# Hourglass attention and a gated feed-forward on one core: batch 0's attention given a fourth PSUM tile, and four smaller edits

## The chip, the cores and the metric

One of the eight cores of a Trainium2 chip runs the whole program. The time is the device's own, in microseconds, from start to end of one execution. The engines are PE (matrix multiply, with its weight loads PEld), ScalarE (ACT), VectorE (DVE), GpSimd (POOL) and SyncE (SP, here only a queue that issues DMAs). Matmul results go to PSUM, 8 banks of 128 partitions x 512 fp32, and are taken from there by ScalarE or VectorE.

## What is computed

q, k and v have 8 batches, 8 heads, 576 tokens and 64 dimensions. Each head gets two attentions, a "down" one over tokens averaged by four (144 x 144) and a local one with a band mask, and their sum goes through a feed-forward of 512 to 2048 to 512 on 4608 tokens:

```python
q_d = q.reshape(B, H, Sd, factor, D).mean(axis=3)
k_d = k.reshape(B, H, Sd, factor, D).mean(axis=3)
v_d = v.reshape(B, H, Sd, factor, D).mean(axis=3)
out_d = sm_attn(q_d, k_d, v_d)
out_up = np.repeat(out_d, factor, axis=2)
...
mask = np.abs(pos[:, None] - pos[None, :]) < factor
scores = scale * np.matmul(q, k.transpose(0, 1, 3, 2))
scores = np.where(mask, scores, -1000000000.0)
...
out_local = np.matmul(attn, v)
return (out_up + out_local).astype(np.float32)
...
h = x @ w_in
g = h * (1.0 / (1.0 + np.exp(-1.702 * h)))
return (g @ w_out).astype(np.float32)
```

Here `sm_attn` is scaled softmax attention, `attn` the softmax of the masked scores, and x the attention's result with the heads side by side.

## The kernel before

The program is written in the order in which each engine is to run it; nothing is reordered. Waits between engines are derived from the tiles that the instructions read and write.

**Batch 0 first (lines 922 to 1018).** No feed-forward work exists yet, so batch 0's attention stands alone. POOL loads q, k and five chunks of v (`load_vb0`, one DMA each, casting to bf16), then, behind a one-element copy `gate` that waits for chunk 1, the weights w_in. PE runs warming matmuls on zeros (`warm`), writes the mask as additive bars (`bars0`), adds scores (`scores0`, heads in quads `qd` 0 and 1), and ScalarE takes the exp (`exp0`). `scores_d` makes the down scores and `exp_down` their exp. `prep_vd_pe` sums v by four with matmuls into PM[0] and PM[1], and VectorE casts the result. Per pair of heads `hp`, `av_local0` and `av_down0` multiply with v into `o[hp]`, `normalise0` divides on VectorE, `transp_sum` turns y with matmuls and sums both attentions, and `copy_x` takes x to SBUF on ScalarE.

**PSUM.** Three tiles PA of two banks each (called PB in another order) and two tiles PM of one bank. Before, `o` uses PB[0], PB[1], PB[2] and again PB[0]; x of pair 0 is turned into the two PM tiles, of pairs 1, 2, 3 into PB[1], PB[2], PB[0]. The first feed-forward matmuls (`part`, `acc`, `late`) then take banks as they come free.

**Groups 0 to 7 (`mm1`, `mm2`).** Each group is 512 tokens. `mm1` makes 16 blocks `ffc` of 128 hidden columns, four matmuls of 128x512 each, into a list of banks, and `silu` (L817) takes each block out on ScalarE. From group 2 on the banks run PM[0], PA, PM[1], PA, PA, and again so, and the last six blocks alternate between PM[0] and PM[1]. Group 1 begins with both halves of two PA tiles. `mm2` sums 16 matmuls per block `t` of 128 tokens into alternating PM tiles (L884), and `store` copies each block out on ScalarE (L869) and sends it from SP's queue. In group 0 blocks 0 and 1 run abreast in the two PM tiles, and 2 and 3 in PB[0].

**Attention of batch g+1** runs inside group g as steps at set places of these loops (`POS`, and `POS_0` for group 0; place n below 16 is before block n of mm1, from 16 on before matmul n-16 of mm2). Step 0 makes scores of quad 0 (`s_pe`), step 1 their exp and mask (`s_act`), step 2 both for quad 1, steps 3 and 4 `avx` for heads (0,1) and (2,3): matmuls into the PA tiles, then Ln and exp on ScalarE (L739 to L745), copies and products on VectorE. Group 0 has four steps `avx1` in place of two.

```python
PA = [psum.tile([128, 2, 512], FP32, name=f"pa{i}") for i in range(3)]
PM = [psum.tile([128, 512], FP32, name=f"pm{i}") for i in range(2)]
two = [PA[i][:, u, :] for i in range(3) for u in range(2)]
bank, abreast = [PM[0], two[0], PM[1], two[2], two[4]], 4
bank = bank + bank + PM + PM + PM
```

Of the kernel before, what the change touches and what calls it, by code (L numbers as in the profile page):

```python
# [8 lines left out]
FP32 = mybir.dt.float32  # L9
# [10 lines left out]
def kernel(  # L20
# [9 lines left out]
    nc = tc.nc  # L30
    B, H, S, D = q.shape
# [22 lines left out]
    psum = ctx.enter_context(  # L54
        tc.tile_pool(name="psum", bufs=1, space=bass.MemoryType.PSUM)
    )
# [6 lines left out]
    vbs = [persist.tile([128, 5, H, 65], BF16, name=f"vb{i}") for i in range(2)]  # L63
# [4 lines left out]
    for _ in range(2):  # L68
        t = work.tile([128, 2 * (S + SD)], FP32, name="l", tag="l", bufs=2).bitcast(BF16)
# [2 lines left out]
    kdT = [persist.tile([128, 160, 2], BF16, name=f"kdT{i}") for i in range(NQ)]  # L72

    PA = [psum.tile([128, 2, 512], FP32, name=f"pa{i}") for i in range(3)]
    PM = [psum.tile([128, 512], FP32, name=f"pm{i}") for i in range(2)]
    PB = [PA[2], PA[0], PA[1]]
    turn = {"a": 2, "m": 0}

    def pm_tile():
        turn["m"] += 1  # L80
        return PM[turn["m"] % 2]

# [93 lines left out]
    def make_up():  # L176
        nc.scalar.copy(out=up, in_=id128[:, :, None].to_broadcast([128, 128, 4]))
# [78 lines left out]
            )  # L256

    def load_vb0(i):
        n = min(128, S - 114 * i)
        nc.gpsimd.dma_start(  # L260
            out=vbs[0][0:n, i, :, 0:D],
            in_=bass.AP(
                tensor=v.tensor, offset=v[0, 0].offset + 114 * i * D,
                ap=[[D, n], [S * D, H], [1, D]],
            ),
        )

    def load_v4(b):
        for kc in range(3):
# [20 lines left out]
    def load_w_out(c):  # L290
        nc.gpsimd.dma_start(
            out=w_out_bf[:, 4 * c : 4 * c + 4, :],
            in_=bass.AP(
                tensor=moe_w_out.tensor, offset=moe_w_out.offset + c * 512 * d_model,
                ap=[[d_model, 128], [128 * d_model, 4], [1, d_model]],
            ),
        )
# [74 lines left out]
    def prep_vd_pe(b, pv, kcs=range(3), eng=None, between=None):  # L372
        vb, vd = vbs[b], vds[b]

        def heads(x, j):
            if b == 0:
                return x.rearrange("p (hp j) d -> p hp j d", j=2)[:, :, j]
            return x.rearrange("p (m u j) d -> p m u j d", m=2, u=2)[:, :, j]

        for kc, iis in ((0, (0, 1)), (1, (1, 2, 3)), (2, (3, 4))):  # L380
            if kc not in kcs:
                continue
            c0 = 256 * (kc - kcs[0])
            for i in iis:
                if between:
                    between(kc, i)
                for j in range(2):
                    nc.tensor.matmul(
                        pv[64 * j : 64 * j + 64, c0 : c0 + D * HP],
                        lhsT=psel[b][i // 4][:, PSEL_AT[i, kc] : PSEL_AT[i, kc] + 64],  # L390
                        rhs=heads(vb[:, i, :, 0:D], j),
                        start=(i == iis[0]), stop=(i == iis[-1]),
                        tile_position=(0, 64 * j),
                    )
        cp = eng.tensor_copy if eng else nc.scalar.copy
        cp(
            out=vd[:, kcs[0] : kcs[-1] + 1, :, 0:D],
            in_=pv[:, 0 : 256 * len(kcs)].rearrange(
                "p (k h d) -> p k h d", k=len(kcs), h=HP
            ),  # L400
        )


    def bank0(r, i):
        if i < 4:
            return PB[r // 2][:, r % 2, Q0 * i : Q0 * i + Q0]
        return (PB[2][:, r, 0:Q0] if r < 2 else PM[r - 2][:, 0:Q0])

# [50 lines left out]
    def scores_d(b, qd, sd=None, rounds=range(6)):  # L459
        bank = [sd[:, u, :] for u in range(2)]  # L460
        for n in rounds:
            kc, a = n // 2, n % 2
            for r in range(4):
                rows = slice(32 * r, 32 * r + 32)
                u, j = (r // 2, r % 2) if b < 1 else (r % 2, r // 2)
                nc.tensor.matmul(  # L466
                    bank[u][64 * j : 64 * j + 64, SD * kc : SD * kc + SD],
                    lhsT=kdT[qd][rows, 48 * kc : 48 * kc + 64, a],
                    rhs=qdT[b, qd][rows, :, a],
                    start=(a == 0), stop=(a == 1),  # L470
                    tile_position=(32 * r, 64 * j),
                )
        return sd
# [8 lines left out]
    def exp0(qd):  # L482
        def part(u, j, i, x):
            out = ez[qd][:, u, :, i, 0:Q0] if j is None else ez[qd][:, u, j, i, 0:Q0]
            nc.scalar.activation(out=out, in_=x, func=AF.Exp, scale=inv_sqrt_d)

        def most(u):
            part(u, None, slice(0, 4), PB[u][:, :, 0 : 4 * Q0].rearrange(
                "p j (i c) -> p j i c", c=Q0))

        part(1, 0, 4, PM[0][:, 0:Q0])
        if qd:
            part(1, 1, 4, PM[1][:, 0:Q0])
            most(0)
# [4 lines left out]
        if not qd:  # L499
            part(1, 1, 4, PM[1][:, 0:Q0])  # L500

    def exp_down(qd, sd):
        nc.scalar.activation(  # L503
            out=eds[qd][:, :, 0:432], in_=sd[:, :, 0:432],
            func=AF.Exp, scale=inv_sqrt_d / 16.0,
        )
# [6 lines left out]
    def av_local0(hp, o, chunks):  # L513
        for i in chunks:
            for j in range(2):
                nc.tensor.matmul(
                    o[:, j, 65 * i : 65 * i + 65],
                    lhsT=ez[hp // 2][:, hp % 2, j, i, :],
                    rhs=vbs[0][:, i, 2 * hp + j, :],
                    start=True, stop=True,  # L520
                )

    def av_down0(hp, o):
        Ed, vd, u = eds[hp // 2], vds[0], hp % 2
        for c in range(2):
            for kc in range(3):
                q0 = SD * kc + 16 * c
                for j in range(2):
                    nc.tensor.matmul(
                        o[:, j, 65 * (5 + c) : 65 * (6 + c)],  # L530
                        lhsT=Ed[64 * j : 64 * j + 48, u, q0 : q0 + 128],
                        rhs=vd[64 * j : 64 * j + 48, kc, hp, :],
                        start=(kc == 0), stop=(kc == 2),
                        tile_position=(64 * j, 0),
                    )

    def y_tiles0():
        return (
            work.tile([128, 7, 2, D], BF16, name="y", tag="y", bufs=4),
            work.tile([128, 2, 7, 1], FP32, name="rc0", tag="rc0", bufs=4),  # L540
        )
# [228 lines left out]
    def warm(n, cols=512, t=None):  # L770
        t = pm_tile() if t is None else t
        for _ in range(n):
            nc.tensor.matmul(
                t[:, 0:cols], lhsT=wz[:, 0:128], rhs=wz[:, 0:cols], start=True, stop=True
            )
# [37 lines left out]
    def new_gT():  # L813
        return moe_sb.tile([128, n_ffc, TG], BF16, name="gT", tag="gT")
# [6 lines left out]
    def mm1(g, gT, steps):  # L821
        two = [PA[i][:, u, :] for i in range(3) for u in range(2)]
        bank, abreast = [PM[0], two[0], PM[1], two[2], two[4]], 4
        if g == 0:
# [85 lines left out]
        for f in steps.get(n, ()):  # L910
            f()

    POS = [12, 16, 35, 43, 54]
    POS_0 = [16, 18, 28, 40, 49, 58, 67]
    VDP_0 = 36

    o, y, x = {}, {}, {}
# [13 lines left out]
    for i in range(5):  # L931
        load_vb0(i)
# [6 lines left out]
        load_qk(1, qd)  # L939
    load_w_out(0)  # L940
    load_w_out(1)
    warm(11)
    make_up()
    make_psel0()
    prep_1("k", 0, 0)
# [25 lines left out]
    scores0(1, 4, (0, 1))  # L971
    exp0(1)
    for hp in range(4):
        o[hp] = PB[hp % 3]
        y[hp] = y_tiles0()
    prep_vd_pe(0, PM[0], (0, 1), eng=nc.vector)
    av_local0(0, o[0], range(3))
    prep_vd_pe(0, PM[1], (2,), eng=nc.vector)
    av_local0(0, o[0], range(3, 5))
    av_local0(1, o[1], range(5))  # L980
    for hp in range(4):
        if hp == 2:
            exp_down(1, scores_d(0, 1, PB[2]))
        if hp > 1:
            av_local0(hp, o[hp], range(5))
        av_down0(hp, o[hp])
        normalise0(o[hp], y[hp])
    make_dm()
    make_mask()
    gT0 = new_gT()  # L990
    acc = PM + [PB[n][:, u, :] for n in (1, 2, 0) for u in range(2)]
    late = [acc[n] for n in (0, 1, 6, 2, 4, 0, 1, 0, 1, 0)]

    def part(ffcs, *dmcs):
        for dmc in dmcs:
            for ffc in ffcs:
                hps_mm(0, ffc, dmc, acc[ffc])

    def turned(hp, n):
        x = PM if n is None else [PB[n][:, u, :] for u in range(2)]  # L1000
        transp_sum(y[hp], x)
        copy_x(0, hp, x)

    turned(0, None)
    turned(1, 1)
    part((0, 1), 0)
    turned(2, 2)
    part((0, 1), 1)
    part((2, 3), 0)
    turned(3, 0)  # L1010
    nc.scalar.preload_act_table_set("silu_and_others")
    part((2, 3), 1)
    part((0, 1, 2, 3), 2)
# [5 lines left out]
    for g in range(n_groups):  # L1019
# [32 lines left out]
        if b < B:  # L1052
            for n, f in zip(POS if g else POS_0, attention(b)):
                steps.setdefault(n, []).append(f)
# [35 lines left out]
```

## Time and profile before

| what | value |
|---|---|
| three runs | 313.64, 313.80, 314.07 us (median 313.80) |
| profiled execution, its own time | 313.58 us |
| its span, first to last instruction | 311.8 us |
| granted PE clock, mean | 1.000 |
| PE matmul 128x512 in L884, mean | 379 ns, one every 216 ns |
| SiLU from PM (L817), mean | 604 ns |
| output copy (L869), mean with its smaller forms | 582 ns |
| first 24.2 us: PE busy | 19.6 us |
| 24.2 to 281.0 us: PE busy | all but 0.07 us |

In the page and the timeline a row gives the start, the length, the engine, the line, what is written and read, how many instructions are merged, and in brackets the engine's idle time before it and what ended that. Matmuls overlap in PE's pipeline: one lasts 379 ns, but the next starts 216 ns after it.

### The profile page before, as it was taken

What the parts mean: (1) busy time and instruction counts of PE and PEld (TensorE: products, weight loads), DVE (VectorE), ACT (ScalarE), POOL (GpSimd) and SP (SyncE); (2) the same over time, 40 slices, a digit from 0 to 9 for tenths busy, and PEclk for the clock granted to TensorE, in tenths of its full rate; (3) what the DMA queues carried; (4) which work ended last, traced back from release to release, by engine and by line L of the source; (5) the groups of instructions that cost most, each with busy time, mean ns of one, the idle gap of its engine ahead of it and who ended that gap; (6) DMA issues with size and microseconds to landing.
All of it is one profiled execution on the core that took longest, in us unless ns stands there. A gap on an engine that the chain in (4) does not pass through costs nothing.

```text
span 311.8 us, 9642 instructions
## 1 busy us (share of the span) xinstructions
PE 303.6 (97%) x4182; PEld 156.6 (50%) x4182; DVE 149.7 (48%) x304; ACT 203.3 (65%) x327; POOL 148.7 (48%) x169
## 2 busy tenths in 40 slices
PE   8789999999999999999999999999999999999995
PEld 3464554674644555455545554555455544444444
DVE  5984937761495059605980389028912770000000
ACT  4737766787767777667866895589558857316611
POOL 8552294295238943795359733983397210000000
PEclk9999999999999999999999999999999999999999
DMA  6999999899537941696159715991430110010011
GB/s 108 135 208 210 182 117 211 218 237 227 139 108 181 201 126 68 177 214 155 46 176 197 191 39 159 189 204 63 133 92 33 39 69 0 34 67 36 0 67 67
DMA packets 64042, 39.93 MB, mean 128 GB/s; under 512 B 44544, under 2 KB 54912, under 8 KB 64000
## 3 DMA queue, kind: packets, MB, share of 16 engines
q0 software_dynamic: 18784, 14.94, 34.2%
q1 hardware_dynamic: 45072, 24.32, 27.8%
q8 instruction: 32, 0.52, 0.7%
q10 hardware_dynamic: 144, 0.07, 0.1%
q14 instruction: 10, 0.08, 0.1%
HBM read 44.81 MB, written 9.44 MB: 174 GB/s over the span
## 4 chain that ended last, share of the span: by engine, by line
PE 92%; DMA 3%; POOL 2%; issue 1%; DVE 1%; ACT 1%; POOLq 0%; DVEq 0%; ACTq 0%
PE pm L884 37%; PE pm L806 25%; PE pa L806 16%; PE pa L439 3%; DMA vb<-in_v_dram 3%; PE pa L884 2%; PE pa L696 2%; PE pa L674 2%; PE pa L466 2%; PE pm L899 1%; POOL vb L260 1%; DVE y L547 1%; PE pa L609 1%; PE pa L567 0%; PE pa L597 0%
## 5 line engine op out<-in xcount | busy, mean ns | idle before, releaser
L884 PE MATMUL pm<-w_out_bf,gT 128*128 128x512 bf16 x528 | 119.4, 379 | 0.0
L806 PEld LDWEIGHTS <-w_in_bf 128*128 128x128 bf16 x612 | 59.2, 98 | 63.1 <-issue 0.3
L806 PE MATMUL pm<-xT,w_in_bf 128*128 128x512 bf16 (+1 forms) x367 | 89.0, 370 | 0.1
L884 PEld LDWEIGHTS <-gT 128*128 128x128 bf16 x560 | 52.8, 98 | 62.4 <-issue 0.6
L817 ACT ACTIVATE gT<-pm 128x512 bf16<-128x512 f32 x88 | 52.7, 604 | 39.7 <-PE pm L806 39.7
L511 DVE TENSOR_TENSOR es<-es,mask 128x600 bf16<-128x600 bf16 x28 | 18.4, 692 | 85.1 <-ACT es L477 84.9
L806 PE MATMUL pa<-xT,w_in_bf 128*128 128x512 bf16 (+1 forms) x245 | 59.0, 361 | 0.0
L869 ACT ACTIVATE osb<-pm 128x512 f32<-128x512 f32 (+2 forms) x35 | 20.3, 582 | 29.2 <-PE pm L884 26.7
L817 ACT ACTIVATE gT<-pa 128x512 bf16<-128x512 f32 x56 | 32.1, 610 | 6.3 <-PE pa L806 6.3
L766 POOL TENSOR_TENSOR xT<-xT,od 128x576 bf16<-128x576 bf16 x12 | 17.2, 1432 | 38.7 <-DVE xT L750 38.2
L750 DVE TENSOR_TENSOR xT<-n,l 128x285 bf16<-128x285 f32 (+1 forms) x96 | 28.2, 370 | 0.0
L343 POOL TENSOR_TENSOR pq<-kT 128x576 f32<-128x576 bf16 x11 | 12.8, 1160 | 30.4 <-DVE kT L312 30.4
L871 DVE TENSOR_SCALAR osb<-pm 128x128 f32<-128x128 f32 x1 | 0.3, 292 | 53.5 <-ACT osb L869 53.5
L360 POOL TENSOR_TENSOR pq<-v 112x512 f32<-112x512 f32 x18 | 23.7, 1316 | 3.6 <-DMA v<-in_v_dram 3.6
L312 DVE STREAM_TRANSPOSE kT<-kb 128x576 f32<-128x576 f32 x16 | 20.0, 1248 | 3.9 <-DMA kb<-in_k_dram 3.9
L503 ACT ACTIVATE ed<-pa 128x864 bf16<-128x864 f32 x16 | 14.3, 894 | 9.8 <-PE pa L466 9.8
L312 DVE STREAM_TRANSPOSE qT<-qb 128x576 f32<-128x576 f32 x16 | 19.9, 1242 | 0.4 <-DMA qb<-in_q_dram 0.3
L477 ACT ACTIVATE es<-pa 128x600 bf16<-128x600 f32 x28 | 17.2, 670 | 0.1
L745 ACT ACTIVATE l<-l 128x1440 f32<-128x1440 f32 x12 | 16.8, 1404 | 0.4
L740 DVE COPY n<-pa 128x492 f32<-128x492 f32 x24 | 15.0, 665 | 2.4 <-ACT l L739 1.8
L739 ACT ACTIVATE l<-pa 128x492 f32<-128x492 f32 x24 | 12.6, 578 | 4.4 <-PE pa L696 3.8
L439 PE MATMUL pa<-qT,kT 32*64 32x60 bf16 x1120 | 15.4, 195 | 0.0
(132 smaller groups left out, 354.2 us busy)
## 6 DMA issues: line engine op xcount, KB each, us to landing
out_dram<-osb SPq DMA_DIRECT2D x34, 256.0 KB, 2.1
vf<-in_v_dram SPq DMA_DIRECT2D x60, 128.0 KB, 5.0
v<-in_v_dram SPq DMA_DIRECT2D x72, 96.0 KB, 3.0
kb<-in_k_dram POOLq DMA_DIRECT2D x16, 288.0 KB, 6.8
qb<-in_q_dram POOLq DMA_DIRECT2D x16, 288.0 KB, 8.5
w_out_bf<-in_moe_w_out_dram POOLq DMA_DIRECT2D x4, 512.0 KB, 13.4
w_in_bf<-in_moe_w_in_dram POOLq DMA_DIRECT2D x2, 512.0 KB, 6.7
w_in_bf<-in_moe_w_in_dram POOLq DMA_DIRECT2D x1, 1024.0 KB, 12.6
```

What stands on the lines that cost most here:

```text
L312: nc.vector.transpose(out=t32.rearrange("p (i c) -> p c i", c=18), in_=store[b, qd].bitcast(FP32).rearrange("p (c d) -> p c d", c=18),)
L360: eng.tensor_tensor(out=t1[0:112], in0=x[:, :, 0:2, :], in1=x[:, :, 2:4, :], op=ALU.add)
L439: nc.tensor.matmul(P[1 + r // 2][64 * par : 64 * par + 64, r % 2, 60 * i : 60 * i + 60], lhsT=kT[b, qd][rows, k0 : k0 + 64, a], rhs=qT[b, ...
L477: nc.scalar.activation(out=es[2 * qd + u][:, :, 0:300], in_=sp[u][:, :, 0:300], func=AF.Exp, scale=inv_sqrt_d,)
L511: nc.vector.tensor_tensor(out=ev, in0=ev, in1=mask, op=ALU.mult)
L745: nc.scalar.activation(out=l, in_=l, func=AF.Exp, scale=-1.0)
L750: nc.vector.tensor_tensor(out=out, in0=sub(n, *part), in1=sub(l, *part), op=ALU.mult)
L766: eng.tensor_tensor(out=xs, in0=xs, in1=sub(od[:, u, :], 0, (1, SD), (0, 4)), op=ALU.add)
L806: nc.tensor.matmul(acc[:, c : c + n], lhsT=w_in_bf[:, dmc, ffc * 128 : (ffc + 1) * 128], rhs=xT[dmc][:, g * TG + c : g * TG + c + n], star ...
L817: nc.scalar.activation(out=gT[:, ffc, :], in_=acc, func=AF.Silu, scale=GELU_SCALE)
L869: eng.activation(out=osb, in_=ap, func=AF.Copy, scale=1.0 / GELU_SCALE)
L884: nc.tensor.matmul(ops[t], lhsT=gT[:, ffc, t * 128 : (t + 1) * 128], rhs=w_out_bf[:, ffc, :], start=(ffc == 0), stop=(ffc == n_ffc - 1),)
```

## The change

It makes five edits. PM is no longer two tiles of one bank but the two halves of one tile, PMS, and the fourth pair's `o` is PMS, so that four pairs have four tiles; x is turned into the tile that held the same pair's `o`, and `acc` and `late` are renumbered to name the banks that are free then. The second `scores_d` and `exp_down` move ahead of `av_local0` of pair 1. The last value chunk (120 rows) is loaded by two DMAs of 64 and 56 rows. `warm(11)` becomes `warm(9)`. In groups 1 to 6 the last three steps of `POS` come one matmul sooner.

```diff
-    PM = [psum.tile([128, 512], FP32, name=f"pm{i}") for i in range(2)]
+    PMS = psum.tile([128, 2, 512], FP32, name="pm")
+    PM = [PMS[:, u, :] for u in range(2)]
     PB = [PA[2], PA[0], PA[1]]
...
     def load_vb0(i):
-        n = min(128, S - 114 * i)
-        nc.gpsimd.dma_start(
-            out=vbs[0][0:n, i, :, 0:D],
-            in_=bass.AP(
-                tensor=v.tensor, offset=v[0, 0].offset + 114 * i * D,
-                ap=[[D, n], [S * D, H], [1, D]],
-            ),
-        )
+        rows = min(128, S - 114 * i)
+        for p0 in range(0, rows, 128 if rows == 128 else 64):
+            n = min(rows - p0, 128 if rows == 128 else 64)
+            nc.gpsimd.dma_start(
+                out=vbs[0][p0 : p0 + n, i, :, 0:D],
+                in_=bass.AP(
+                    tensor=v.tensor, offset=v[0, 0].offset + (114 * i + p0) * D,
+                    ap=[[D, n], [S * D, H], [1, D]],
+                ),
+            )
...
-    POS = [12, 16, 35, 43, 54]
+    POS = [12, 16, 34, 42, 53]
...
-    warm(11)
+    warm(9)
...
     for hp in range(4):
-        o[hp] = PB[hp % 3]
+        o[hp] = (PB + [PMS])[hp]
         y[hp] = y_tiles0()
     prep_vd_pe(0, PM[0], (0, 1), eng=nc.vector)
     av_local0(0, o[0], range(3))
     prep_vd_pe(0, PM[1], (2,), eng=nc.vector)
     av_local0(0, o[0], range(3, 5))
+    exp_down(1, scores_d(0, 1, PB[2]))
     av_local0(1, o[1], range(5))
     for hp in range(4):
-        if hp == 2:
-            exp_down(1, scores_d(0, 1, PB[2]))
         if hp > 1:
...
-    acc = PM + [PB[n][:, u, :] for n in (1, 2, 0) for u in range(2)]
-    late = [acc[n] for n in (0, 1, 6, 2, 4, 0, 1, 0, 1, 0)]
+    acc = [t[:, u, :] for t in PB + [PMS] for u in range(2)]
+    late = [acc[n] for n in (6, 7, 0, 2, 4, 6, 7, 6, 7, 6)]
...
-    def turned(hp, n):
-        x = PM if n is None else [PB[n][:, u, :] for u in range(2)]
+    def turned(hp):
+        x = [o[hp][:, u, :] for u in range(2)]
         transp_sum(y[hp], x)
         copy_x(0, hp, x)

-    turned(0, None)
-    turned(1, 1)
+    turned(0)
+    turned(1)
     part((0, 1), 0)
-    turned(2, 2)
+    turned(2)
     part((0, 1), 1)
     part((2, 3), 0)
-    turned(3, 0)
+    turned(3)
```

## The prediction

> **What bounds the kernel now.** I read the page's busy times first, then the chain of waits, then the groups, and then the timeline of each engine around the places that the diff touches. From the page:
>
> ```profile
> PE 303.6 (97%) x4182; PEld 156.6 (50%) x4182; DVE 149.7 (48%) x304; ACT 203.3 (65%) x327; POOL 148.7 (48%) x169
> ...
> PE 92%; DMA 3%; POOL 2%; issue 1%; DVE 1%; ACT 1%; POOLq 0%; DVEq 0%; ACTq 0%
> ...
> L817 ACT ACTIVATE gT<-pm 128x512 bf16<-128x512 f32 x88 | 52.7, 604 | 39.7 <-PE pm L806 39.7
> ```
>
> PE sets the time. After 22.14 us its matmuls follow each other without a gap over 0.07 us; only the first 22 us hold real waits. So an edit can save at most what the prologue wastes, and anything that makes PE wait in the long part costs in full. The last row says why PE never waits there: ScalarE's SiLU always waits for PE, because PE fills the other PM bank meanwhile. The timeline of ScalarE in the last group:
>
> ```profile
> 290.10 0.60 ACT L817 ACTIVATE gT<-pm 128x512 bf16<-128x512 f32 x1 [0.27 <-PE pm L806]
> 290.96 0.60 ACT L817 ACTIVATE gT<-pm 128x512 bf16<-128x512 f32 x1 [0.27 <-PE pm L806]
> ```
>
> One SiLU each 0.86 us, which is four matmuls of 0.216: reading one PM bank overlaps filling the other.
>
> The wait that the prologue edit is about, in the timeline of all engines:
>
> ```profile
> 17.38 0.58 PE L466 MATMUL pa<-qdT,kdT 32*64 32x144 bf16 x24
> ...
> 18.01 0.89 ACT L503 ACTIVATE ed<-pa 128x864 bf16<-128x864 f32 x1 [2.24 <-PE pa L466]
> ...
> 18.95 0.47 PE L516 MATMUL pa<-vb,l 128*128 128x65 bf16 x10 [0.99 <-ACT ed L503]
> ```
>
> PE stands 0.99 us while the second down scores go through the exp.
>
> **The part that decides: PM becomes one tile of two banks.** Are waits set by bank or by tile? The two-bank PA tiles answer. In avx1 ScalarE takes Ln from bank 1 of a tile (L631) and VectorE copies bank 0 of the same tile (L636). They share no element. ScalarE's timeline:
>
> ```profile
> 55.69 0.54 ACT L631 ACTIVATE l<-pa 128x444 f32<-128x444 f32 x1 [0.59 <-PE pa L609]
> 56.98 0.42 ACT L631 ACTIVATE l<-pa 128x300 f32<-128x300 f32 x1 [0.75 <-DVE n L636]
> 57.43 0.82 ACT L642 ACTIVATE l<-l 128x744 f32<-128x744 f32 x1
> 58.27 1.28 ACT L646 ACT_TABLE_LOAD   x1
> 59.56 1.08 ACT L869 ACTIVATE osb<-pm 128x512 f32<-128x512 f32 x2
> ```
>
> The second Ln waits 0.75 us for VectorE's copy out of the other bank. So does avx: VectorE's L740 starts at 82.17, just after ScalarE's L739 (82.13) has left the other bank, though VectorE was free at 81.89. And group 1 puts ffc 0 and 2 into the halves of one PA tile: ffc 0's last matmul ends at 62.12, yet its SiLU starts at 62.59, just after ffc 2's last one (62.55). Reads against reads and reads after writes wait by tile. I take it that writes after reads do too; no row shows PE itself held by the other bank, because today's code never lets two halves of a tile follow each other in that way.
>
> With PMS as one tile, PE's first write into a PM bank waits for every earlier ScalarE read of either. **One such turn, S**: last matmul 0.379 (row of L884) + 0.04 until the SiLU starts (103.39 to 103.43) + SiLU or output copy 0.60 + 0.05 back to PE (ed exp's end 18.90 to matmul 18.95) - 0.216, the slot that would have passed anyway = 0.85 us. Where a table load or the softmax lies ahead of the read on ScalarE's in-order queue, PE waits for that too. By stage:
>
> Group 0 (mm1, mm2). ffc 7 waits for SiLU 6, which queues behind SiLUs 0 to 5: it ends at 31.50 now, 31.70 with SiLU 0 waiting for ffc 1 of its tile; PE is ready at 29.71: 2.0. ffc 12 to 15: 4 S = 3.4. First down matmul: hidden under the scores of step 0. Matmul 52 of mm2 (t=1, after t=0 was stored): PE is there at 55.80, and the store's copy, behind avx1's Ln, exp and table load (lines above), ends near 60.16: 4.4. Sum 9.8.
>
> Group 1. ffc 5 (PM[0]) after SiLU 4 (PM[1]): 62.83 against 65.16: 2.3. ffc 10, 11, 13, 14, 15: 5 S = 4.25 (ffc 12's turn is hidden by 1.0 us of scores). mm2: t=0 one S, 0.85; t=1 one turn, 0.87; t=2 and t=3 wait for output copies behind avx's softmax. PE's timeline of group 1, then ScalarE's:
>
> ```profile
> 81.67 2.55 PE L884 MATMUL pm<-w_out_bf,gT 128*128 128x512 bf16 x11
> 85.23 5.79 PE L884 MATMUL pm<-w_out_bf,gT 128*128 128x512 bf16 x26
> ```
> ```profile
> 84.39 0.58 ACT L869 ACTIVATE osb<-pm 128x512 f32<-128x512 f32 x1
> ...
> 89.36 0.60 ACT L869 ACTIVATE osb<-pm 128x512 f32<-128x512 f32 x1
> ```
>
> The first copy ends 3.35 after PE leaves avx(0,1) at 81.67, and PE has six matmuls to do (1.30): 2.05. The second ends 4.78 after 85.23, with eleven matmuls to do (2.37): 2.4. Sum of group 1: 12.7.
>
> Groups 2 to 6, each: first matmul behind the copy of t=3, 0.85; ffc 5 behind SiLU 2, 0.75 (SiLU 0 now waits for ffc 2, its tile's other bank, then three SiLUs at 0.48 spacing against four matmuls); ffc 11, 13, 14, 15: 3.4; mm2 as above 0.85 + 0.87 + 2.05 + 2.4. Sum 11.2, times five 55.9.
>
> Group 7 (no attention): 0.85 + 0.75 + five S + four S in mm2 + 0.63 for the half-width last copy (0.38 instead of 0.60) = 9.9.
>
> Together 9.8 + 12.7 + 55.9 + 9.9 = **88.3 us**. ScalarE's 65% becomes part of the path.
>
> **The other parts.** *Second down scores sooner, four AV tiles*: without new waits they save 0.99 less about 0.1; AV of pair 0 comes 0.58 later, so VectorE's four normalisations (1.28 each, back to back from 17.38) become the limit at pairs 2 and 3. But the PM tile brings waits here too: warm(4) into PM[0] now waits for the exp part out of PM[1], 11.12 instead of 8.95; that puts the first down exp at about 13.5 (12.41), exp0(1) one us later, the vd sums behind it at 14.9 (14.04), and chunk 2 of them behind VectorE's cast of the first, 16.6. Followed down to the fourth turn of x, I get 23.9 against 24.19: -0.3. Bounds: -0.9 (all of it kept) and +1.0 (the exp's delay passed on).
>
> *Last value chunk in two loads*: POOL issues 0.92 per load at L260 and 0.68 for 64 rows at L249, so 0.44 more on its queue, hidden by its 3.27 of idle ahead of the gate at 12.76 (without that cover 0.44 on w_in, which is needed at 22.14 and was let on at 19.06). All later POOL loads move one place back, and so does the load whose landing each waits for. Same bytes, both halves are needed by the same matmuls; between 0.9 earlier (right with chunk 3, 15.13) and 0.7 later (one more load's issue) than 16.04, and the cast at 16.6 covers most of it: 0.
>
> *Two warming matmuls fewer*: 2 x 0.43 earlier, then PE waits for qT at 8.30 in any case: 0. Spacing fell from 0.43 to 0.2 near 6.1; the bars still fill PE past that. If the rise were missed, the bars and scores to 9.1 would take about 1.0 longer.
>
> *Steps one matmul earlier* (POS): the scores' exp has 0.45 of slack (109.94 to 110.39); avx(0,1)'s PA bank is free only 0.05 before use (112.95, 113.00), but its exp waits 1.06 for PE, so it moves along, and vd (112.70) hangs on VectorE work that moves too: 0, at worst 18 x 0.216 = 3.9. The 0.2 more cover per copy stands in the sums above.
>
> **Sum.** Span 311.8 + 88.3 - 0.3 = 399.8; 1.8 lies around the span in the profiled execution (313.58), which stands 0.2 under the median, so **402 us**.
>
> **Rivals.**
> *Banks are told apart for PE's writes* (the change does what it says): then nothing is added in the groups, the prologue keeps -0.9, and vd of batch 2 (its loads come by SP's queue; it ends at 79.62) meets avx(0,1), which would ask for it at 80.58 - 0.22 - 0.9 = 79.46, giving back up to 0.2: about 312.9. For it: no row shows PE held that way. Against it: the three rows above, in both other directions. It decides from PE's first turn, ffc 7 of group 0. The Trainium skill's page PSUM — Partial Sum Buffer (PSUM bank collisions raise a hardware error) says that engines on different banks run clean; by that the chip asks for no wait and this rival's time would stand. The trace shows that the program waits all the same.
>
> *The clock falls too*: PE would be idle about half the time in ffc 11 to 15. The page shows 1.00 throughout, but no stretch idle like that. At the early spacing (0.427 against 0.216) 20 matmuls in each of 8 groups add 34: 436. The Trainium skill, TensorE: Matmul & The Clock Gate (A second HAM failure mode: psum-queue depth-cycling), tells of such a swing between half and full clock; nothing before shows it.
>
> *Results are readable before the modelled end of a matmul*: 0.16 less on some 56 turns, 393.
>
> **How the numbers follow.** Forecast (with the 393 variant) 79%, clock 11%, banks apart 8% (1 of it with the prologue's gain lost), stalls half covered by something I don't see 2%. The range 388 to 425 takes in S shorter by 0.2, the prologue's bounds, 4 us from POS and part of the clock's loss. Faster by over 0.2% (about what can be told from no change) 7%, within 1%, slower 92%.
>
> **What would show it.** Right: SiLU rows (L817) unchanged in length while PE's idle is some 90 us, released by ScalarE's L817 and L869; a SiLU every 1.7 us in ffc 13 to 15; group 0's PE standing 4 us near the first output copy. Wrong: PE still at 97%, or matmul spacing over 0.216 in the groups (clock).

## The result, and the profile after

| | before | changed |
|---|---|---|
| median | 313.93 us (6 runs, 313.49 to 314.56) | 422.09 us (6 runs, 417.70 to 423.52) |
| ratio | 1 | 1.342, 95% interval 1.335 to 1.349 |
| profiled execution, its span | 313.58, 311.8 | 422.32, 420.5 |
| granted PE clock, mean | 1.000 | 0.970 |

The kernel became a third slower. The page of the changed kernel (a line of after is the line of before plus 3, in part plus 1 or 2; in the groups the columns are busy us, mean ns of one, and the idle time before them with what ended most of it):

```profile
PE 328.0 (78%) x4180; PEld 158.1 (38%) x4180; DVE 144.5 (34%) x304; ACT 205.4 (49%) x327; POOL 148.9 (35%) x170
...
PEclk9999996899989998999999989999999989999999
...
PE 65%; ACT 24%; issue 7%; DVE 2%; DMA 1%; POOL 0%; ACTq 0%; DVEq 0%; POOLq 0%
...
L887 PE MATMUL pm<-w_out_bf,gT 128*128 128x512 bf16 x528 | 130.8, 396 | 42.2 <-ACT osb L872 36.7
L809 PE MATMUL pm<-xT,w_in_bf 128*128 128x512 bf16 (+1 forms) x359 | 94.0, 372 | 39.8 <-ACT gT L820 34.9
...
L820 ACT ACTIVATE gT<-pm 128x512 bf16<-128x512 f32 x86 | 51.5, 599 | 84.8 <-PE pm L809 83.9
```

PE went from 97% to 78%. Its matmuls into pm now stand idle 42.2 and 39.8 us, where before they had 0.0 and 0.1, and it is ScalarE that ends these waits, by the output copy and the SiLU. SiLU itself did not become longer (599 ns); it waits for PE twice as long as before. So both engines wait for each other in turn. PE's timeline in group 7, and ScalarE's:

```profile
357.55 1.02 PE L809 MATMUL pm<-xT,w_in_bf 128*128 128x512 bf16 x4 [0.69 <-ACT gT L820]
359.26 1.02 PE L809 MATMUL pm<-xT,w_in_bf 128*128 128x512 bf16 x4 [0.69 <-ACT gT L820]
360.97 1.02 PE L809 MATMUL pm<-xT,w_in_bf 128*128 128x512 bf16 x4 [0.69 <-ACT gT L820]
362.68 3.61 PE L887 MATMUL pm<-w_out_bf,gT 128*128 128x512 bf16 x16 [0.69 <-ACT gT L820]
```
```profile
358.61 0.60 ACT L820 ACTIVATE gT<-pm 128x512 bf16<-128x512 f32 x1 [1.11 <-PE pm L809]
360.32 0.60 ACT L820 ACTIVATE gT<-pm 128x512 bf16<-128x512 f32 x1 [1.11 <-PE pm L809]
```

Four matmuls, SiLU, four matmuls, SiLU: one block each 1.71 us instead of 0.864, though the blocks alternate between two banks. That is 0.85 us a turn. The longest wait is in group 0 (PE, then ScalarE):

```profile
61.71 0.39 PE L887 MATMUL pm<-w_out_bf,gT 128*128 128x512 bf16 x1
66.34 1.44 PE L887 MATMUL pm<-w_out_bf,gT 128*128 128x512 bf16 x3 [4.25 <-ACT osb L872]
```
```profile
63.56 0.82 ACT L645 ACTIVATE l<-l 128x744 f32<-128x744 f32 x1
64.40 1.28 ACT L649 ACT_TABLE_LOAD   x1
65.70 0.60 ACT L872 ACTIVATE osb<-pm 128x512 f32<-128x512 f32 x1
```

The copy that PE waits for queues behind an exp and a table load. The three matmuls that follow show 1.44 us instead of 0.81: there the clock stood at half.

Time per group, from the first matmul of its mm1 to that of the next, in group 8 to the end of the last matmul. The fourth column is PE's busy time at half clock in the changed kernel; the last is the experiment with fills, below, in which the clock did not fall in the groups:

| group | before | changed | at half clock | with fills |
|---|---|---|---|---|
| 0 | 36.26 | 49.14 | 4.96 | 46.18 |
| 1 | 32.46 | 49.36 | 6.83 | 46.13 |
| 2 | 32.42 | 45.23 | 3.41 | 43.42 |
| 3 | 32.44 | 43.40 | 0 | 43.54 |
| 4 | 32.35 | 45.09 | 3.41 | 43.55 |
| 5 | 32.34 | 43.53 | 0 | 43.51 |
| 6 | 32.33 | 45.07 | 3.41 | 43.39 |
| 7 | 27.63 | 36.98 | 0 | 36.98 |
| 8 | 27.86 | 36.95 | 0 | 36.95 |
| sum | 286.1 | 394.7 | 22.0 | 383.7 |

There are nine groups (4608 / 512), 0 to 8; the description of the kernel and the prediction count only eight. The two without attention are 7 and 8.

The prologue, which four of the five edits are about, gained nothing. VectorE's and PE's rows of the changed kernel:

```profile
16.02 0.69 DVE L399 CAST vd<-pm 128x512 bf16<-128x512 f32 x1 [0.61 <-PE pm L391]
18.74 0.25 DVE L549 RECIPROCAL rc<-pa 128x14 f32<-128x14 f32 x1 [1.09 <-PE pa L532]
...
22.58 0.23 DVE L549 RECIPROCAL rc<-pm 128x14 f32<-128x14 f32 x1
```
```profile
16.76 0.42 PE L391 MATMUL pm<-vb,psel 128*64 128x256 bf16 x4 [0.49 <-DVE vd L399]
...
24.36 0.62 PE L570 MATMUL pm<-up,y 128*128 128x231 bf16 x4
```

The third sum of v (into one half of PMS) waits 0.49 us for VectorE's cast out of the other half. The first normalisation starts at 18.74 (17.38 before), the other three follow at the pace of VectorE, and the fourth turn of x begins at 24.36, where before it began at 24.19.

### The profile page after: what moved, and what is told of

The parts are those of the page before. It is cut to its first block, busy times and chain, and to the rows that moved or that the text cites. A ratio compares the mean times of both kernels' runs of the same rounds, so it can differ in the third digit from the quotient of the medians.

```text
span 420.5 us, 9627 instructions
## 1 busy us (share of the span) xinstructions
PE 328.0 (78%) x4180; PEld 158.1 (38%) x4180; DVE 144.5 (34%) x304; ACT 205.4 (49%) x327; POOL 148.9 (35%) x170
## 3 DMA queue, kind: packets, MB, share of 16 engines
q1 hardware_dynamic: 45072, 24.32, 20.7%
## 4 chain that ended last, share of the span: by engine, by line
PE 65%; ACT 24%; issue 7%; DVE 2%; DMA 1%; POOL 0%; ACTq 0%; DVEq 0%; POOLq 0%
PE pm L887 24%; PE pm L809 20%; ACT gT L820 10%; PE pa L809 10%; ACT osb L872 5%; PE pa L442 2%; ACT l L742 2%; ACT L750 2%; PE pa L469 1%; PE pa L677 1%; ACT l L744 1%; PE pa L887 1%; DMA qb<-in_q_dram 1%; PE pa L699 1%; PE pm L902 1%
## 5 line engine op out<-in xcount | busy, mean ns | idle before, releaser
L887 PE MATMUL pm<-w_out_bf,gT 128*128 128x512 bf16 x528 | 130.8, 396 | 42.2 <-ACT osb L872 36.7
L809 PE MATMUL pm<-xT,w_in_bf 128*128 128x512 bf16 (+1 forms) x359 | 94.0, 372 | 39.8 <-ACT gT L820 34.9
L887 PEld LDWEIGHTS <-gT 128*128 128x128 bf16 x560 | 54.8, 101 | 116.6 <-issue 63.7
L820 ACT ACTIVATE gT<-pm 128x512 bf16<-128x512 f32 x86 | 51.5, 599 | 84.8 <-PE pm L809 83.9
L514 DVE TENSOR_TENSOR es<-es,mask 128x600 bf16<-128x600 bf16 x28 | 12.6, 471 | 170.3 <-ACT es L480 169.7
L809 PE MATMUL pa<-xT,w_in_bf 128*128 128x512 bf16 (+1 forms) x253 | 61.4, 366 | 0.0
L769 POOL TENSOR_TENSOR xT<-xT,od 128x576 bf16<-128x576 bf16 x12 | 18.1, 1510 | 104.1 <-DVE xT L753 103.5
L820 ACT ACTIVATE gT<-pa 128x512 bf16<-128x512 f32 x58 | 33.1, 605 | 12.3 <-PE pa L809 12.3
L363 POOL TENSOR_TENSOR pq<-v 112x512 f32<-112x512 f32 x18 | 22.8, 1264 | 12.9 <-DMA v<-in_v_dram 12.9
L346 POOL TENSOR_TENSOR pq<-kT 128x576 f32<-128x576 bf16 x11 | 12.8, 1160 | 33.0 <-DVE kT L315 33.0
## 6 DMA issues: line engine op xcount, KB each, us to landing
w_out_bf<-in_moe_w_out_dram POOLq DMA_DIRECT2D x4, 512.0 KB, 13.7
```

What stands on the lines that cost most here:

```text
L363: eng.tensor_tensor(out=t1[0:112], in0=x[:, :, 0:2, :], in1=x[:, :, 2:4, :], op=ALU.add)
L769: eng.tensor_tensor(out=xs, in0=xs, in1=sub(od[:, u, :], 0, (1, SD), (0, 4)), op=ALU.add)
L809: nc.tensor.matmul(acc[:, c : c + n], lhsT=w_in_bf[:, dmc, ffc * 128 : (ffc + 1) * 128], rhs=xT[dmc][:, g * TG + c : g * TG + c + n], star ...
L820: nc.scalar.activation(out=gT[:, ffc, :], in_=acc, func=AF.Silu, scale=GELU_SCALE)
L887: nc.tensor.matmul(ops[t], lhsT=gT[:, ffc, t * 128 : (t + 1) * 128], rhs=w_out_bf[:, ffc, :], start=(ffc == 0), stop=(ffc == n_ffc - 1),)
```

## The experiments

**The merge by itself.** The kernel before with one edit:

```diff
-    PM = [psum.tile([128, 512], FP32, name=f"pm{i}") for i in range(2)]
+    PMS = psum.tile([128, 2, 512], FP32, name="pm")
+    PM = [PMS[:, u, :] for u in range(2)]
```

> The kernel before, with PM as two halves of one tile PMS and nothing else changed. Theory (a wait is set by the tile, so every turn between PM[0] and PM[1] costs PE one drain and one ScalarE read): all stalls of the changed kernel stay, 97.7 us in nine groups, and the older step places add 0.22 us at each of two copies in six groups, 2.6 us; with 9 to 12 us of half clock 423 to 427 us. Rival (banks are told apart, another of the edits costs the time): 313.9 us.

Measured: 422.55 us (421.73 to 422.69, 3 runs; a fourth took 430.58), ratio 1.344 (1.334 to 1.355). The merge is the whole loss. Attention groups without half clock took 43.82 to 43.97 us, against 43.40 and 43.53 in the changed kernel: the steps placed one matmul sooner do give back about 0.4 us a group, two slots of 0.216, where two output copies are waited for. The fourth turn of x began at 24.84, so the change's other edits earn 0.48 us of the prologue back.

**Everything but the merge.** PM stays two tiles, the fourth pair's o is PB[0] again and x goes where it went before; the split load, the sooner down scores, `warm(9)` and the sooner steps are kept. Of the diff, the sooner down scores:

```diff
+    exp_down(1, scores_d(0, 1, PB[2]))
     av_local0(1, o[1], range(5))
     for hp in range(4):
-        if hp == 2:
-            exp_down(1, scores_d(0, 1, PB[2]))
```

> Two PM tiles as before, pair 3's AV in PB[0] as before; of the change only the last chunk in two loads, the second down scores sooner, two warming matmuls fewer and the steps one matmul sooner. Theory: none of these costs; the 0.99 us wait for the down exp goes, about half of it comes back because pair 3 then waits for VectorE to have normalised pair 0: 313.3 to 313.6 us, PE's gaps in the groups stay under 0.1 us. Rival (one of them costs): over 314.5 us.

Measured: 313.86 us (313.03 to 314.82, 12 runs), ratio 0.9984 (0.9956 to 1.0012). No gap in a group is over 0.07 us, but there is no measurable gain either (313.3 to 313.6 were expected). PE's timeline shows why the prologue earns nothing:

```profile
15.55 0.30 PE L390 MATMUL pm<-vb,psel 128*64 128x256 bf16 x2 [1.01 <-DMA vb<-in_v_dram]
...
19.62 0.47 PE L518 MATMUL pa<-vb,l 128*128 128x65 bf16 x10 [0.49 <-DVE y L549]
```

The wait for the exp (0.99 us before) is down to 0.10. In its place PE waits 0.57 us longer than before for value chunk 3 (1.01 against 0.44), and 0.49 us until VectorE has read pair 0 out of the tile that pair 3 reuses.

**The change with the merged tile for batch 0 only.** PMS comes from a pool that is closed once x is turned; two one-bank tiles then take its space.

```diff
+    pms_pool.close()
+    PM[:] = [pm_pool.tile([128, 512], FP32, name=f"pm{i}") for i in range(2)]
+    acc[6:8] = PM
```

> The whole change, but PMS is given back after pair 3's x has been turned and its two banks become two tiles PM[0] and PM[1] for all groups. Theory: the groups have no waits and no half clock any more, the prologue is that of the changed kernel (fourth turn of x 0.2 us later than before): 314.0 us, 313.7 to 314.4. Rival (four tiles for AV or the renumbered banks cost the time): over 400 us.

Measured: 314.90 us (313.44 to 315.80, 12 runs), ratio 1.0026 (1.0006 to 1.0047). The same matmuls and SiLUs on two separate tiles have no gap in the groups, and 107 us are gone. PSUM has eight banks and all are in use, so these are the same two banks: the wait belongs to the tile. PE's timeline in group 7, where the changed kernel stood 0.69 us at each block:

```profile
261.66 4.91 PE L812 MATMUL pm<-xT,w_in_bf 128*128 128x512 bf16 x22
```

What is left, +0.3%, is a little more than expected and goes with the clock: four executions with a granted clock of 1.000 took 313.44 to 314.07 us, eight with 0.992 to 0.995 took 314.75 to 315.80. The profiled one is among the four, so where the clock fell in the others is not shown. The two versions with fills and with four tiles, below, have the same start; in their profiled executions the clock stood at half for one stretch of 3.41 us there (12.30 to 15.71 and 10.77 to 14.18).

**The same, with the two early writes moved out of PMS.** The two writes into PMS that wait there for a reader of its other half go elsewhere.

```diff
-    warm(4, t=PM[0])
+    warm(4, t=PB[2][:, 0, :])
-    prep_vd_pe(0, PM[1], (2,), eng=nc.vector)
+    prep_vd_pe(0, PB[1][:, 0, :], (2,), eng=nc.vector)
```

> As the one before, and batch 0 avoids the merged tile's waits too: the four warming matmuls behind the first scores go to PB[2], the third part of the v sums to PB[1]. Theory: the 2.07 us wait of the warming matmuls and the 0.49 us wait for VectorE's cast go, the scores' order then gives what it promised: 0.6 to 0.9 us under the kernel before, 313.0 to 313.3 us. Rival (VectorE's four normalisations are the limit in any case): 313.8 us, as the kernel before.

Measured: 313.70 us (312.97 to 314.61, 12 runs), ratio 0.9981 (0.9955 to 1.0008). The fourth turn of x starts at 23.83, so 0.36 us of gain, held up by the load once more.

```profile
15.56 0.31 PE L394 MATMUL pm<-vb,psel 128*64 128x256 bf16 x2 [0.83 <-DMA vb<-in_v_dram]
```

The time is nearer to the rival's 313.8 us than to the expected 313.0 to 313.3. What it gains on the version above is mostly the clock: nine of its twelve executions had 0.998 or more, with a median of 313.58 us, and the four such executions above have 313.64.

**Four tiles in groups 7 and 8.** The change, with another order of banks there:

```diff
+            if g > 6:
+                bank = ([PM[0], two[0], two[2], two[4]] * 4)
```

> The change, but mm1 of groups 7 and 8 turns over four banks of four different tiles (the first half of the merged tile, and the first halves of PA's three tiles) in place of its sixteen of before. Theory (the loss is PE's wait for ScalarE's read of the same tile, 0.85 us a turn): with four tiles no write meets a read of its own tile that is less than three results old, so the five turns of ffc 11 to 15, the wait before ffc 5 and the one at the first write of mm2 go, some 5.6 us in each of the two groups, from 36.98 and 36.95 to about 31.3; the whole kernel 411 us (409 to 413), less or more by what the clock does in the other groups. Rival (PE waits for something else that the merge brings, such as the bank order or ScalarE being late by itself): both groups stay at 36.9 and the kernel at 421.

Measured: 407.30 us (405.87 to 411.91, 4 runs), ratio 1.297 (1.289 to 1.305). Groups 7 and 8 went from 36.98 and 36.95 to 31.37 and 31.34, by the expected 5.6 each. PE's timeline in group 7:

```profile
350.97 1.03 PE L809 MATMUL pm<-xT,w_in_bf 128*128 128x512 bf16 x4
351.83 2.75 PE L809 MATMUL pa<-xT,w_in_bf 128*128 128x512 bf16 x12
354.42 1.03 PE L809 MATMUL pm<-xT,w_in_bf 128*128 128x512 bf16 x4
```

Matmuls into pm now follow those into pa without an idle time, since three blocks lie between two writes to one tile. Its mm2 was left alone and kept its turns of 0.68 and 0.73 us. So the wait is for a recent reader of the same tile, not for a ScalarE that is late by itself. The median lies below the expected 409 to 413 because the clock fell less in most executions: the profiled one took 411.91 us at a mean clock of 0.967, the other three 405.87 to 407.52 at 0.978 to 0.983.

**Fills in the longest waits.** The change, with matmuls whose results nobody reads, in front of matmul 52 of group 0's mm2, ffc 5 of group 1 and matmul 48 of groups 1 to 6:

```diff
+            if g == 0 and n == 52:
+                warm(12, t=PB[1][:, 0, :])
+            if 0 < g < 7 and n == 48:
+                warm(6, t=PA[0][:, 0, :])
...
+            if g == 1 and ffc == 5:
+                warm(8, t=PA[2][:, 0, :])
```

> The change, with matmuls of 128x512 on the warming tile, whose results nobody reads, put into the long waits of PE: 12 (2.6 us) into the 4.25 us before matmul 52 of group 0's mm2, 8 (1.7 us) into the 2.2 us before ffc 5 of group 1, 6 (1.3 us) into the 1.9 to 2.2 us before matmul 48 of groups 1 to 6. Theory (the granted clock falls where a window of 3.41 us is idle for some two thirds, which only these waits bring about): the fills lie inside the waits, no stretch at half clock is left, and the 11.0 us that half clock cost come back: 411 us (410 to 414). Rival (the half-idle ffc 11 to 15, or PE's mean load, brings the clock down, and the long waits only happen to lie beside it): the falls stay, 419 to 424 us. The waits themselves should end when they did, since ScalarE and the vector work in front of it are untouched.

Measured: 411.99 us (410.93 to 412.41, 4 runs), ratio 1.308 (1.301 to 1.316). With 12.1 us of useless work more on PE (56 matmuls of 0.216) the kernel is 10.1 us faster than the changed one. The page's row of the clock, and PE where it had stood 4.25 us:

```profile
PEclk9899999999999999999999999999999999999999
```
```profile
63.93 2.75 PE L776 MATMUL pa<-wz 128*128 128x512 bf16 x12 [1.80 <-ACT l L634]
66.70 1.02 PE L893 MATMUL pm<-w_out_bf,gT 128*128 128x512 bf16 x4
```

In the prologue it stood at half from 12.30 to 15.71, behind a wait of 2.08 us that the merged tile brings there and that got no fill (the warming matmuls of `warm(4)` wait for the exp's read of the other half). After that the clock does not fall any more up to the last instruction. ffc 11 to 15 are as idle as they were, so they do not bring it down.

**The last value chunk in one load.** The version with the early writes moved out, with the kernel before's `load_vb0`.

> The version with the merged tile for batch 0 alone and both early writes moved out of it, but batch 0's last value chunk loaded in one piece, as in the kernel before. Theory (the split is worth nothing: the last chunk landed at 16.03 in two loads and at 16.04 in one, and one issue of 0.7 us on POOL fewer lets the loads behind it start sooner): 313.7 as with the split, or up to 0.3 us less (313.3 to 313.8), the fourth turn of x starting at 23.6 to 23.9. Rival (the second load takes its share of the queues earlier, and the first half is what the sum of v waits for): 0.2 to 0.5 us more, 313.9 to 314.2.

Measured: 314.35 us (313.33 to 315.05, 12 runs), ratio 0.9996 (0.9972 to 1.0020). The start came out better than expected, the time worse, though the two versions' ratios overlap: mm1 starts at 21.34 (22.14 before) and the fourth turn at 23.48, yet the span is 0.7 longer. Over all profiled executions the last chunk landed at 15.58 to 16.06 in one load (five of them) and at 15.91 to 16.37 in two (six): the split brings nothing. Where the lead of 0.8 us went, in the timelines of POOL, of VectorE, and of ScalarE and PE in this version:

```profile
51.04 0.17 POOL L924 CAST vf<-w_out_bf 1x1 f32<-1x1 bf16 x1 [4.07 <-DMA w_out_bf<-in_moe_w_out_dram]
51.18 1.20 POOL L664 TENSOR_TENSOR xT<-xT,od 128x576 bf16<-128x576 bf16 x1
```
```profile
51.25 1.30 DVE L653 TENSOR_TENSOR od<-n,l 128x144 f32<-128x144 f32 x1 [0.81 <-ACT l L646]
```
```profile
54.04 0.42 ACT L635 ACTIVATE l<-pa 128x300 f32<-128x300 f32 x1 [1.42 <-DVE n L640]
```
```profile
54.51 0.25 PE L601 MATMUL pa<-ed,vd 48*64 48x144 bf16 x2 [0.42 <-ACT l L635]
...
60.43 0.59 PE L810 MATMUL pm<-xT,w_in_bf 128*128 128x512 bf16 x3 [0.40 <-ACT osb L873]
```

POOL's add stands behind a cast that waits for a transfer, so it starts at 51 however early PE is. VectorE's product, now earlier, meets it and takes 1.30 us instead of 0.31. VectorE's next copy is late by that, ScalarE's Ln waits 1.42 us for the copy (0.42 before), and PE waits 0.42 and 0.40 for what ScalarE does next. At 60.43 PE is 0.22 us behind the kernel before, so these waits account for 1.0 of the 1.5 us lost from the start to the end; the rest goes in shorter stops.

**That cast issued later.** The version above, and the kernel before as a control, each with:

```diff
-            load_v(2, gate=after(w_out_bf[0:1, 12, 0:1], nc.gpsimd))
...
+                steps[POS_0[3]].append(
+                    lambda: load_v(2, gate=after(w_out_bf[0:1, 12, 0:1], nc.gpsimd))
+                )
```

> The version with the merged tile for batch 0 alone, both early writes moved out of it and the last value chunk in one load, whose mm1 starts 0.80 us sooner than before (21.34 against 22.14) and whose time is nevertheless that of before. Edit: the one-element cast on POOL that holds batch 2's value loads back until a w_out chunk has landed is issued behind the first pair of batch 1's attention instead of ahead of group 0. Theory: POOL's add of that pair (1.20 us) sits behind the cast, whose release at 51 is fixed by the transfer; in the run before it fell on DVE's od (1.30 us in place of 0.31 at 51.25) and the 1 us came out as PE's waits of 0.42 at 54.51 and 0.40 at 60.43. With the cast behind it the add runs near 49.4 beside DVE's copies out of PSUM, od takes 0.31 again, both waits go: 313.6 (313.1 to 313.9), 0.5 to 0.8 less than the version without the edit. Rival (the attention of batch 1 is bound by other work at a fixed time, its loads or w_out): the waits stay or move, and the time stays within 0.2 of 314.2.

> The kernel before with the same single edit (the cast that holds batch 2's value loads is issued behind the first pair of batch 1's attention). There POOL's add (50.92 to 52.12) ended just before DVE's od (52.03, 0.31 us) and PE had no wait in group 0 or 1. Theory: nothing to gain, 313.8 (313.5 to 314.1); its use is to say whether the edit by itself costs anything, the loads of batch 2's values being issued at 51 in both. Rival (the add at 49.4 slows DVE's copies or the strided products beside it): up to 0.5 us more.

Measured: 313.33 us (312.70 to 314.74, 12 runs), ratio 0.9984 (0.9966 to 1.0002); the control 313.77 us (313.25 to 316.47, 12 runs; another took 318.83), ratio 1.0003 (0.9982 to 1.0024). The median is 1.0 us under that of the version above, but the intervals of the two ratios overlap. In the profiled execution (314.62 us, one of the longer ones) the collision is gone (the product takes 0.31 us at 51.94) and so are both waits, but two others stand in their place:

```profile
49.01 0.38 PE L888 MATMUL pm<-w_out_bf,gT 128*128 128x512 bf16 x1 [0.85 <-DMA w_out_bf<-in_moe_w_out_dram]
...
81.54 0.26 PE L678 MATMUL pa<-ed,vd 48*64 48x144 bf16 x4 [0.54 <-POOL vd L367]
```

PE arrives before a chunk of w_out has landed (48.97; it was 47.16 before and 47.37 in the version above), and later before batch 2's vd is ready. The first of these takes PE's whole lead before the place of the collision, so this trace does not show that the two old waits went because of the edit. So no version tried is faster than the kernel before by more than the measurement can tell; the two best medians (313.33 and 313.70) have intervals that hold 1.

## Why the prediction was right, and what its number missed

The mechanism was right: slower, because the halves of one tile wait for each other's readers. It was argued from rows in which no write of PE occurred, and PE's turns (1.71 us a block), the merge alone (422.55) and the merge undone in the groups (314.90) show it. What it left open, whether PE's writes wait by tile too, was decided at the first turn: PE stood 1.90 us before ffc 7 of group 0, until ScalarE had read the other half.

**S and the terms by group.** S of 0.85 us is what PE's rows show (1.71 - 0.864). Freed of the half clock (the table's column with fills less that of before), the groups lost 9.9, 13.7, then 11.0 to 11.2 in each of groups 2 to 6, where the prediction had 9.8, 12.7 and 11.2. The table counts the wait before a group's first matmul, 0.85, with the group ahead of it, where the prediction counts it with the group itself; put back, group 1 lost 12.8 and group 8 9.9. The wait at matmul 52 of group 0 was 4.25 + 0.165 of drain (4.4 predicted), those of ffc 5 of group 1 and of t=2 and t=3 were 2.21, 1.88 and 2.23 + 0.165 each (2.3, 2.05 and 2.4 predicted).

**The number was 20 us short: 402 against 422,** inside the range of 388 to 425 but near its end. That it lies inside is in part luck: the range took in some of the clock's loss, but nothing for a miscounted group, and the three errors all went the same way. The span grew by 108.7 us, not 88.0. Three terms make the 20.7:

- *The count of groups*, 9.3 us. "Group 7 (no attention)" is two groups; they lost 9.35 and 9.09, and the prediction has one. With nine groups its own terms sum to 88.3 + 9.3 = 97.6; without half clock the nine lost 97.6. The description of the kernel has the same error ("Groups 0 to 7").
- *The clock*, 11.0 us: 22.0 us of PE work at half clock cost half of that; the fills gave 10.1 us of it back in the medians. The rival "the clock falls too" was held at 11% and placed in ffc 11 to 15, for 34 us. It came true at another place: there the clock never fell, but it did at the waits of two microseconds and more that the prediction itself had worked out.
- *The prologue*, 0.4 us: mm1 began 0.1 us later, not 0.3 sooner. The waits that the prediction followed are there (first down exp at 13.79, 13.5 predicted; third sum of v at 16.76, 16.6 predicted); the step that failed is the last one, down to the fourth turn of x, at 24.36 instead of 23.9.

**Edits costed at nothing.** The split load: right, no gain. `warm(9)`: the versions without the merge show no sign of a cost, though it was never run alone. The sooner steps: 0.4 us a group under the merge, as the sums had it, and no gap over 0.07 us in any group where they ran without it on two tiles (everything but the merge). (The prediction's 19.06 for w_in is the issue of a w_out load; w_in's first part landed at 18.78. Nothing hangs on it.)

**The other rivals.** "Banks are told apart" fell at the first turn, and its 312.9 was also too good for the case that it described: with separate tiles in the groups the rest of the change took 314.90 us, and 313.70 with the early writes moved, where PE's rows show chunk 3's landing taking part of the prologue's gain. "Readable before the modelled end" fell as well: a turn is the full 0.85.

## What to carry to other kernels

Before two buffers are merged into one allocation, look for rows in which two engines touch different parts of an allocation that exists already: if one waits for the other, the merge turns a double buffer into a single one, and every turn costs the whole read behind the write. A tile that one stage wants to be wide can be wide for that stage only. And a sub-microsecond gain at the start of a kernel has to be followed to the next event with a time of its own, such as a landing transfer: here the landings of value chunk 3 and of w_out took much of it, one after the other.

## What the runs showed of the hardware

**In the groups, a window that is three fifths idle was enough for the clock to fall.** In the changed kernel and in the merge alone every stretch at half clock inside the groups was 3.41 us long, or two in a row, on a grid with one fixed period. Windows of the changed kernel, then of the merge alone (columns: from:to, length, then busy time and count of PE, its weight loads, VectorE, ScalarE, POOL, and the granted clock, DMA share, GB/s):

```profile
61.07:64.48 3.41, 1.03 (x37) 0.61 (x30) 2.19 (x8) 2.02 (x5) 1.21 (x1) 1.00 0.38 84
64.48:67.89 3.41, 1.55 (x4) 0.56 (x4) 3.38 (x8) 1.80 (x2) 0.18 (x1) 0.50 0.20 76
...
112.26:115.68 3.42, 1.19 (x7) 0.47 (x5) 3.00 (x12) 2.39 (x3) 0.00 (x0) 1.00 0.03 13
115.68:119.09 3.41, 3.41 (x10) 1.22 (x9) 3.41 (x5) 0.00 (x0) 1.41 (x2) 0.50 0.17 64
201.01:204.42 3.41, 1.81 (x9) 0.71 (x8) 2.99 (x9) 3.35 (x5) 1.09 (x1) 1.00 0.00 0
204.42:207.84 3.42, 2.79 (x13) 1.27 (x13) 3.42 (x9) 0.58 (x1) 0.00 (x0) 1.00 0.20 77
...
356.43:359.84 3.41, 2.04 (x10) 0.77 (x8) 0.00 (x0) 1.20 (x2) 0.00 (x0) 1.00 0.00 0
```
```profile
73.84:77.26 3.42, 1.34 (x13) 1.05 (x11) 0.00 (x0) 2.48 (x5) 2.15 (x1) 1.00 0.85 189
...
104.57:107.98 3.41, 1.31 (x7) 0.48 (x5) 2.79 (x9) 2.48 (x4) 0.00 (x0) 1.00 0.00 1
107.98:111.39 3.41, 3.41 (x93) 2.18 (x92) 2.14 (x6) 0.81 (x2) 3.01 (x2) 0.50 0.22 81
292.29:295.71 3.42, 1.39 (x7) 0.68 (x7) 3.32 (x11) 1.95 (x3) 0.00 (x0) 1.00 0.16 64
```

At full clock, a window of the grid in the groups with PE busy for 1.34 of 3.41 us or less was followed by one at half clock (that of 73.84 by one from 77.26 on); one with 1.39, 1.81 or 2.04 was not. The busy times rest on modelled ends, so the bound near 0.4 is good to a few per cent. It does not hold for the prologue with its many small matmuls: in the control's profiled execution (318.83 us) a window there with PE busy for 1.75 us (12.14 to 15.55) was followed by four at half clock, in which PE was busy for 2.42 to 3.41 us. PE's busy time alone does not decide there, and what does is not shown. The same wait of 2.2 us thus costs nothing more when the edge of a window cuts it (204.42) and 1.7 us when it lies inside one (115.68). The times of one program's executions go with it: the changed kernel's took 417.7 to 423.5 us, the shortest at a mean clock of 0.978, the longest at 0.966. The Trainium skill, TensorE: Matmul & The Clock Gate (What's actually happening), gives the window as 3413 ns and free-running; the trace agrees, with 3.41 us. It has the clock fall after at least one idle window; by the rows here the window need not be idle throughout.

**A product of two SBUF operands on VectorE was held up by POOL's add**: 1.30 us instead of 0.31 (the rows above), to 0.17 us behind the add's end at 52.38. The kernel before has more such rows: the product with the mask (L511, 128x600) took 0.47 us in all 16 rows without a POOL instruction beside it, and 0.99 to 1.23 us in ten of the twelve with one. The Trainium skill, SBUF — State Buffer (SBUF: two separate sides), calls the port pair that both use an exclusive lock that is held for a whole instruction, against VectorE operations with two SBUF inputs too; the rows agree but for the two of the twelve that were not held up.
